# Loads and stores shared by two issuing engines, weight low bits also on GpSimd, and one pair of keys instead of four transposed by TensorE

## The chip, the cores and the metric

The kernel runs on one core of a Trainium2 chip. The core has TensorE (PE, matrix products into PSUM; PEld is its weight load), VectorE (DVE), ScalarE (ACT), GpSimd (POOL) and SyncE (SP), each with its own instruction stream that runs in program order; they wait for each other on semaphores. DMA transfers are issued from the streams of SP, ACT and POOL and carried out by 16 DMA engines. The metric is the device time of one execution in microseconds (us), smaller is better.

## The reference

Block-sparse attention (4 batches, 8 heads, 768 positions, head size 64) is followed by a two-layer network over 3072 tokens:

```python
scores = scale * np.matmul(q, k.transpose(0, 1, 3, 2))      # mask: window, edges, sampled blocks
attn = np.exp(scores - max); attn /= (sum + 1e-09)
x = np.matmul(attn, v)  ->  (3072, 512)
h = x @ w_in                                                # 512 x 2048
g = np.maximum(h, 0.0) + alpha * np.minimum(h, 0.0)
out = g @ w_out                                             # 2048 x 512
```

`moe_w_in` and `moe_w_out` arrive as 64-bit floats (the kernel loads them as pairs of 32-bit words), the rest as 32-bit floats.

## The kernel before, in words

**Precision.** Each operand is written as a sum of two 16-bit floats, a high part (`times`: scale and round) and a low part (`rest`: scale and subtract the high part), and a product is three TensorE products. Before that the 64-bit weights are turned into 32-bit ones in three steps per tile of 128 by 512 (32 tiles, 16 of `w_in`, 16 of `w_out`): `emit_n1` on DVE shifts the high word left by three, `emit_n2` brings in the three low bits, `emit_n3` on DVE merges. `emit_n2` is either one DVE instruction (L813) or one ACT instruction on single bytes (L811).

**Attention.** A unit is one pair of heads for 256 query rows, and it has four score steps (192 in all, 48 units). A step is: scores on PE (`emit_s`, four matmuls, L559), mask and row maximum on DVE (`emit_bias`, L569), exponential on ACT (`emit_exp`, L576), the row sum's reciprocal (L580, L584), the high part of the probabilities P on any of three engines (L348, L350, L352), the low part on POOL in two instructions (L358, L359) or on DVE in one (L356), and a transpose of both parts by one DMA that SP issues (`emit_p_t`, L599). When four steps are done, `emit_av` (36 matmuls, L634) multiplies with V. Keys are transposed too: for the first batch by TensorE (`emit_k_pe`, with copies out of PSUM by `emit_k_copy` on ACT or DVE), for the others by DMA (`emit_k_t`), with a second copy whose halves are swapped (`emit_k_swap`, two DMAs).

**Network.** For each chunk of 256 tokens (12 chunks) there are 8 up groups (`emit_up`, 24 matmuls, L948) and 8 down groups (`emit_down`, 12 matmuls, L987), with the activation on DVE (L958, L959), its high part on ACT (L964) and its low part on POOL (L969). The first down group needs the scale of all of `w_out`, so all its tiles must have gone through the three steps.

**What sets the order.** The kernel lists all operations with a priority, the engines that may do each, a duration guessed for each engine, and the buffers it takes. `Plan.run` plays a list schedule over them: it starts the ready operation of lowest priority number on the engine that would end it first, and lets transfers pass through two rings (SP's and ACT's). The order that comes out is the program order of all engines, and it is fixed. So a changed guess or buffer count moves instructions everywhere. Priorities of the weights are `V_WI`, `W_WI`, `V_WO`, `W_WO` (start and step per tile), of the network `MOE_LAG` and `MOE_BOOST`, of the first values `PL_V` and `P_V`; `BUFS` has the buffer counts; `PL` is a repeating string that says which engine makes the low part of P in a step (`g` POOL, `v` DVE); `LQ` has the engines that may issue loads.

Of the kernel before, what the change touches and what calls it, by code (L numbers as in the profile page):

```python
# [14 lines left out]
ALU = mybir.AluOpType  # L15
# [12 lines left out]
MOE_LAG = 9.585  # L28
MOE_BOOST = 5.593
V_WI = -1.832  # L30
W_WI = 0.74
V_WO = -2.974
W_WO = 1.2
WI_LO = "pe"
PL_V = -24.873
P_V = 3.807
PL = "ggv"
LD = 5
P_PE = 0
RAWP = ["x", "wr"]  # L40
K_PE = 1
Q_PE = 1
BUFS = {"wr": 1, "vf": 4, "qf": 4, "qt": 3, "qn": 2, "ph": 5, "e": 4, "pt": 4, "x": 2, "g": 3, "junk": 2, "sid": 2, "kt": 4, "ks": 4, "v2": 4, "gh": 3, "gl": 3}
# [16 lines left out]
class Plan:  # L60
# [4 lines left out]
    SHARE = {"SP": 0.3, "ACT": 0.7}  # L65
# [15 lines left out]

    def run(self):
        now, left = 0.0, len(self.ops)
        idle = dict.fromkeys(self.ENGINES, 0.0)
# [11 lines left out]
        events = []  # L96
        rings = {"SP": [], "ACT": []}
# [30 lines left out]
        while left:  # L128
            progress = True
            while progress:  # L130
# [4 lines left out]
                for o in ready:  # L135
                    if any(not b.live and all(self.free[x] <= 0 for x in b.pools) for b in o.alloc):
                        continue
# [47 lines left out]
            for _, _, kind, o in due:  # L185
                if kind == "dma":
                    rings["SP" if o.eng == "SP" else "ACT"].append([1.15 * o.dma, o])
                elif kind == "fin":
                    finish(o)
# [5 lines left out]
def attn_moe(ctx: ExitStack, tc: tile.TileContext, q, k, v, sampled, w_in, w_out, alpha, out):  # L195
    nc = tc.nc
# [165 lines left out]
    LQ = {"ACT": 0.06}  # L362
    MAX4 = {"DVE": (0.55, 0), "ACT": 0.85, "POOL": 1.05}
    LOW4 = {"DVE": (0.94, 0), "POOL": (1.05, 1.65)}
# [290 lines left out]
    def prep_k(b, hp, prio, gate, pl):  # L655
# [12 lines left out]
        if b == 0 and K_PE:  # L668
# [7 lines left out]
        o_kt[b, hp] = [plan.op(prio - 2, {"SP": 2.4}, lambda: emit_k_t(b, hp), [o], [kbuf[b, hp]], [nb], dma=2.3)]  # L676
        o_ks[b, hp] = [plan.op(prio - 2, {"SP": 0.12}, lambda e: emit_k_swap(e, b, hp), o_kt[b, hp],
# [21 lines left out]
    def prep_q(c, prio, pl, gate):  # L699
# [16 lines left out]
        for u, fb in zip(us, fbs):  # L716
# [12 lines left out]
            o_qt[u] = plan.op(p - 2, {"SP": 0.8 * f}, lambda u=u: emit_q_t(u), [o], [qtbuf[u]], [nb], dma=0.75 * f)  # L729

    def attend(n):
# [12 lines left out]
        lo = {"POOL": (1.05, 1.65)} if PL[n % len(PL)] == "g" else {"DVE": (0.94, 0)} if PL[n % len(PL)] == "v" else LOW4  # L744
# [10 lines left out]
        o_pt[n] = [plan.op(n - 1, {"SP": 2.4}, lambda: emit_p_t(n), [o], [ptbuf[u, h]], [pb], dma=2.2)]  # L755
# [52 lines left out]
    def emit_n2(e, name, f, h):  # L808
        r, d, byte = raw_of(name, f, h)
        if e == "ACT":  # L810
            nc.scalar.activation(byte[:, :, 4], byte[:, :, 3], AF.Copy, scale=1.0 / 32, bias=-31.0 / 64)  # L811
        else:
            nc.vector.scalar_tensor_tensor(d, low_of(name, f, h), 29, d, ALU.logical_shift_right, ALU.bitwise_or)  # L813
        T["mask", name, f, h] = 7 - (1 << 30) if e == "ACT" else -(1 << 30)
# [291 lines left out]
```

## Time and profile before

| | |
|---|---|
| median of the runs | 878.76 us (fastest 878.57) |
| profiled execution, its own time | 879.08 us |
| its span, first to last instruction | 877.1 us |
| PE / DVE / ACT / POOL busy | 802.9 / 692.0 / 546.0 / 550.2 us |
| mean granted clock of TensorE | 0.963 of full |
| DMA issues on ACT / SP | 136 loads and stores / 248 transposes and 24 swaps |

The profiled execution's own time is 2.0 us more than its span and 0.3 us from the median. The profile cuts the span into 40 slices and gives each engine's busy share of every slice; it lists groups of equal instructions with their mean duration, stretches of time with each engine's busy time, and the instructions in order of time.

### The profile page before, as it was taken

Reading aid. Unit: us, or ns where it says so; the run is one execution under the profiler, and the core shown is the slowest. Engines: PE = TensorE matmul, PEld = TensorE weight load, DVE = VectorE, ACT = ScalarE, POOL = GpSimd, SP = SyncE. Lnnn points to the kernel's source line nnn. Section 1 sums busy time; section 2 is a strip of 40 time slices with the busy share of each in tenths; the row PEclk is TensorE's granted clock in tenths of the full one; section 3 lists DMA queues with packets and bytes.
Section 4 is the critical chain, followed back from the end, with each engine's and each line's share of the span. In section 5 each row is a group of like instructions: output and inputs, shape, how many; then the busy total and the mean of one; then the engine's idle time right before and its main releaser. Section 6 shows DMA issues by size and latency. Waiting matters only on the chain.

```text
span 877.1 us, 17172 instructions
## 1 busy us (share of the span) xinstructions
PE 802.9 (92%) x6249; PEld 534.4 (61%) x6249; DVE 692.0 (79%) x1413; ACT 546.0 (62%) x1178; POOL 550.2 (63%) x446
## 2 busy tenths in 40 slices
PE   3865656899999999999999999999999999999997
PEld 2522323666675666666666667666766766676664
DVE  4999998999887877678888797789797888775322
ACT  5787767678756676765857656477568555564111
POOL 3387556696845877565846776666567666566121
PEclk9876976999999999999999999999999999999999
DMA  7877789576898888977979889777989777766000
GB/s 236 240 180 192 168 180 203 129 134 133 177 208 169 160 149 139 202 140 138 210 157 201 131 145 182 150 140 159 214 151 175 146 133 125 115 125 105 13 25 25
DMA packets 381844, 133.80 MB, mean 153 GB/s; under 512 B 346404, under 2 KB 375104, under 8 KB 381760
## 3 DMA queue, kind: packets, MB, share of 16 engines
q1 hardware_dynamic: 345728, 90.74, 61.2%
q10 hardware_dynamic: 35968, 41.95, 16.3%
q8 instruction: 49, 0.80, 0.4%
q14 instruction: 35, 0.29, 0.1%
q0 software_dynamic: 64, 0.02, 0.0%
HBM read 35.67 MB, written 6.29 MB: 48 GB/s over the span
## 4 chain that ended last, share of the span: by engine, by line
PE 64%; DVE 18%; issue 6%; ACT 3%; DMA 2%; POOL 1%; ACTq 1%; POOLq 0%; DVEq 0%
PE o L987 22%; PE h L948 22%; PE sp L559 11%; PE av L634 9%; DVE e L569 4%; DVE ph L356 2%; DMA kf<-in_k_dram 2%; DVE wo L818 1%; DVE wo L813 1%; ACT e L576 1%; DVE v L356 1%; DVE g L958 1%; DVE wo L356 1%; DVE wo L806 1%; ACT ph L348 1%
## 5 line engine op out<-in xcount | busy, mean ns | idle before, releaser
L948 PE MATMUL h<-x,wi 128*128 128x256 f16 x2304 | 269.4, 274 | 0.0
L948 PEld LDWEIGHTS <-wi 128*128 128x128 f16 x2304 | 225.9, 98 | 39.1 <-issue 1.7
L987 PE MATMUL o<-wo,gh 128*128 128x512 f16 x768 | 229.8, 381 | 1.3 <-DVE wo L356 1.3
L359 POOL TENSOR_TENSOR ph<-e,ph 128x768 f16<-128x768 f32 x128 | 223.0, 1742 | 10.7
L576 ACT ACTIVATE e<-e,nm 128x768 f32<-128x768 f32 x192 | 178.3, 929 | 79.3 <-DVE nm L569 75.1
L569 DVE CUSTOM_DVE_ANT_0 e<-sp,bias,cs 128x768 f32<-128x768 f32 x192 | 190.5, 1007 | 24.7 <-PE sp L559 23.2
L358 POOL TENSOR_SCALAR e<-e,rs 128x768 f32<-128x768 f32 x128 | 134.3, 1049 | 113.9 <-ACT ph L348 63.1
L969 POOL TENSOR_TENSOR gl<-g,gh 128x512 f16<-128x512 f32 x96 | 119.8, 1249 | 101.6 <-ACT gh L964 97.1
L964 ACT CAST gh<-g 128x512 f16<-128x512 f32 x96 | 59.1, 616 | 145.3 <-DVE g L959 128.1
L987 PE MATMUL o<-wo,gl 128*128 128x512 f16 x384 | 146.1, 380 | 1.0 <-POOL gl L969 1.0
L958 DVE TENSOR_SCALAR g<-h,am 128x256 f32<-128x256 f32 x192 | 83.7, 477 | 74.8 <-PE h L948 72.3
L559 PEld LDWEIGHTS <-qt 128*128 128x128 f16 x768 | 74.3, 101 | 90.7 <-issue 36.5
L559 PE MATMUL sp<-kt,qt 128*128 128x512 f16 (+1 forms) x384 | 98.3, 339 | 30.0 <-DVE nm L569 23.7
L987 PEld LDWEIGHTS <-gh 128*128 128x128 f16 x768 | 74.7, 98 | 79.2 <-issue 2.9
L348 ACT ACTIVATE ph<-e,rs 128x768 f16<-128x768 f32 x106 | 97.7, 928 | 15.7 <-DVE rs L584 15.3
L634 PE MATMUL av<-pt,v 128*64 128x256 f16 x1728 | 104.8, 276 | 1.7 <-DVE nm L569 1.7
L634 PEld LDWEIGHTS <-v 128*64 128x64 f16 x1728 | 91.6, 111 | 22.1 <-issue 17.0
L559 PE MATMUL sp<-ks,qt 128*128 128x512 f16 (+1 forms) x384 | 98.7, 340 | 0.0
L356 DVE SCALAR_TENSOR_TENSOR ph<-e,rs,ph 128x768 f16<-128x768 f32 x64 | 82.6, 1291 | 4.9 <-ACT ph L348 4.7
L959 DVE SCALAR_TENSOR_TENSOR g<-h,gsc,g 128x512 f32<-128x512 f32 x96 | 72.1, 751 | 3.4
L987 PEld LDWEIGHTS <-gl 128*128 128x128 f16 x384 | 37.7, 98 | 49.6 <-POOL gl L969 2.8
L352 POOL TENSOR_SCALAR ph<-e,rs 128x768 f16<-128x768 f32 x35 | 35.3, 1008 | 50.7 <-DVE rs L584 37.6
(131 smaller groups left out, 752.1 us busy)
## 6 DMA issues: line engine op xcount, KB each, us to landing
wo<-in_moe_w_in_dram ACTq DMA_DIRECT2D x16, 512.0 KB, 5.8
raw<-in_moe_w_out_dram ACTq DMA_DIRECT2D x16, 512.0 KB, 4.3
kf<-in_k_dram ACTq DMA_DIRECT2D x16, 384.0 KB, 4.6
qf<-in_q_dram ACTq DMA_DIRECT2D x48, 128.0 KB, 3.3
vf<-in_v_dram ACTq DMA_DIRECT2D x16, 384.0 KB, 5.5
out_dram<-ob ACTq DMA_DIRECT2D x24, 256.0 KB, 4.2
ks<-kt SPq DMA_DIRECT2D x24, 192.0 KB, 3.8
pt<-ph SPq DMA_TRANSPOSE x192, 4.1
```

The costliest lines, as they stand in the source:

```text
L348: nc.scalar.activation(dst, src, AF.Copy, scale=scale)
L356: nc.vector.scalar_tensor_tensor(dst, src, scale, hi, ALU.mult, ALU.subtract)
L358: nc.gpsimd.tensor_scalar(tmp, src, scale, 1.0, ALU.mult, ALU.mult)
L359: nc.gpsimd.tensor_tensor(dst, tmp, hi, ALU.subtract)
L559: nc.tensor.matmul(T["sp", n][:, a:z], T["qt", u][:, h, i, :], kt[:, h, a:z], start=(x == 0), stop=(x == 1))
L569: nc.vector.tensor_tensor_reduce(T["e", n], T["sp", n], bias[:, t0 + j % w, :], scale=T["cs", c][:, hp : hp + 1], scalar=3.0e38, op0=ALU.a ...
L576: nc.scalar.activation(T["e", n], T["e", n], AF.Exp, bias=T["nm", n], scale=-1.0, accum_out=T["su", n])
L634: nc.tensor.matmul(av[h * D : (h + 1) * D, : n * P], v2[:, h, t, vv, :], T["pt", u, h][:, pl * NT + t, :], start=(m == 0), stop=(m == len( ...
L948: nc.tensor.matmul(ph[:, i, :], win(w, f, ct), x[:, ct, :], start=(m == 0), stop=(m == len(terms) - 1))
L958: nc.vector.tensor_scalar(g[:, i, :], ph[:, i, :], 0.0, am1[:, f : f + 1], ALU.min, ALU.mult)
L969: nc.gpsimd.tensor_tensor(T["gl", c, j], T["g", c, j], T["gh", c, j], ALU.subtract)
L987: nc.tensor.matmul(T["o", c][t], g[:, i, t * P : (t + 1) * P], wout(w, f), start=(f == 0 and m == 0), stop=(f == NF - 1 and m == 2),)
```

## The change

Four things are changed together.

1. Loads and stores may be issued by SP or by ACT, whichever the planner finds free (before: by ACT alone). Transposes stay on SP.
2. The low bits of a weight tile may also be made on POOL.
3. Only the first of the four key pairs of batch 0 is transposed by TensorE; the other three go by DMA on SP like those of later batches. The probabilities of the first four steps are transposed by TensorE (`P_PE`, before by DMA).
4. The planner's numbers are set anew: priorities, guesses, buffer counts (`wr` 1 to 2, `vf` 4 to 5; `qt` 3 to 2, `ph` 5 to 4, `pt` 4 to 3), and `PL` from "ggv" to "gv", so that every second step instead of every third has its low part of P on DVE.

```diff
-MOE_LAG = 9.585
-MOE_BOOST = 5.593
-V_WI = -1.832
-W_WI = 0.74
-V_WO = -2.974
-W_WO = 1.2
+MOE_LAG = 10.759
+MOE_BOOST = 3.497
+V_WI = -0.008
+W_WI = 0.663
+V_WO = 0.327
+W_WO = 0.625
 WI_LO = "pe"
-PL_V = -24.873
-P_V = 3.807
-PL = "ggv"
+PL_V = -37.055
+P_V = -5.132
+PL = "gv"
-P_PE = 0
-RAWP = ["x", "wr"]
+P_PE = 4
+RAWP = ["wr", "x"]
 K_PE = 1
+N2P = 1.0
...
-    SHARE = {"SP": 0.3, "ACT": 0.7}
+    SHARE = {"SP": 0.5, "ACT": 0.5}
...
-    LQ = {"ACT": 0.06}
+    LQ = {"SP": 0.47, "ACT": 0.5}
...
-        if b == 0 and K_PE:
+        if b == 0 and hp < K_PE:
...
+        elif e == "POOL":
+            nc.gpsimd.tensor_scalar(byte[:, :, 4], byte[:, :, 3], 1.0 / 32, -31.0 / 64, ALU.mult, ALU.add)
...
-        o = plan.op(p, {"ACT": 1.27, "DVE": (0.6, 0)}, lambda e, f=f: emit_n2(e, "wi", f, 0), [o])
+        o = plan.op(p, {"ACT": 1.27, "DVE": (0.65, 0), "POOL": N2P}, lambda e, f=f: emit_n2(e, "wi", f, 0), [o])
...
-            plan.op(stop - MOE_BOOST, {"ACT": 0.06}, lambda e, t=t: emit_store(e, c, t), [o], [], [ob], dma=0.8)
+            plan.op(stop - MOE_BOOST, LQ, lambda e, t=t: emit_store(e, c, t), [o], [], [ob], dma=0.8)
```

The start of ACT's stream before (`kf` are keys, `qf` queries as loaded, `wo<-in_moe_w_in` a raw tile of `w_in`, which is kept in the space of `wo`; `junk` is the output of a sum of squares):

```order
L238 ACTIVATE warm<-ones 128x1
L388 DMA kf<-in_k_dram 128x2x384
L388 DMA qf<-in_q_dram 128x2x128 x4
L388 DMA kf<-in_k_dram 128x2x384 x3
L388 DMA wo<-in_moe_w_in_dram 128x4x256 x5
L344 ACTIVATE junk,kss<-kf 128x768
```

and now:

```order
L251 ACTIVATE warm<-ones 128x1
L401 DMA qf<-in_q_dram 128x2x128 x2
L401 DMA kf<-in_k_dram 128x2x384 x2
L401 DMA wo<-in_moe_w_in_dram 128x4x256 x2
L357 ACTIVATE junk,ssq<-qf 128x256
L357 ACTIVATE junk,kss<-kf 128x768
```

Thirteen issues stood ahead of ACT's first sum of squares, now six do. SP's stream began with twelve transposes of P (`pt<-ph`); now it begins with loads, and the keys' transposes (`kt<-kn`) and swapped copies (`ks<-kt`) stand between further loads:

```order
L401 DMA wo<-in_moe_w_in_dram 128x4x256 x3
L481 DMA_TRANSPOSE kt<-kn 128x12x128
L401 DMA wo<-in_moe_w_in_dram 128x4x256
L401 DMA qf<-in_q_dram 128x2x128
L481 DMA_TRANSPOSE kt<-kn 128x12x128
L401 DMA qf<-in_q_dram 128x2x128 x2
L401 DMA wo<-in_moe_w_in_dram 128x4x256 x4
L401 DMA ks<-kt 64x1536 x2
L481 DMA_TRANSPOSE kt<-kn 128x12x128
```

A load that stands behind a transpose there is issued only after the wait of that transpose. On POOL the first work behind the constants was the high parts of keys, queries and P:

```order
L299 TENSOR_SCALAR nident<-ident 128x128
L352 TENSOR_SCALAR kn<-kf,ks 128x12x64
L352 TENSOR_SCALAR qn<-qf,sq 128x4x64 x2
L352 TENSOR_SCALAR ph<-e,rs 128x768
L358 TENSOR_SCALAR e<-e,rs 128x768
L359 TENSOR_TENSOR ph<-e,ph 128x768
```

and is now the low bits of the first weight tiles (L826, in the space of `wo`):

```order
L312 TENSOR_SCALAR nident<-ident 128x128
L826 TENSOR_SCALAR wo<-wo 128x512 x4
L884 TENSOR_SCALAR sid<-ident,ssc 128x128
L826 TENSOR_SCALAR wo<-wo 128x512
```

Five of the eighteen low-bit operations that POOL does in the new order have moved ahead of its first P.

## Rows read from the trace of the kernel before

**Rows 1.** The page: busy time of each engine; granted clock in 40 slices.

```profile
PE 802.9 (92%) x6249; PEld 534.4 (61%) x6249; DVE 692.0 (79%) x1413; ACT 546.0 (62%) x1178; POOL 550.2 (63%) x446
PEclk9876976999999999999999999999999999999999
```

**Rows 2.** Windows: stretch, length, busy us (instructions) by engine, clock, DMA share, GB/s.

```profile
0.00:24.00 24.00, 9.72 (x69) 6.59 (x70) 11.09 (x43) 13.35 (x28) 8.55 (x26) 1.00 0.74 235
24.00:150.00 126.00, 79.71 (x449) 41.81 (x448) 118.80 (x225) 92.23 (x211) 80.54 (x59) 0.77 0.83 193
150.00:214.00 64.00, 59.64 (x472) 40.31 (x471) 60.48 (x119) 46.28 (x100) 44.14 (x33) 0.95 0.66 132
214.00:840.00 626.00, 621.12 (x5054) 425.08 (x5053) 491.83 (x1012) 389.15 (x834) 410.04 (x323) 1.00 0.83 151
```

**Rows 3.** Timeline of PE: start, duration, instructions; first up group, first down group, 41st step.

```profile
148.82 4.93 PE L948 MATMUL h<-x,wi 128*128 128x256 f16 x24
...
174.10 1.06 PE L987 MATMUL o<-wo,gh 128*128 128x512 f16 x2
...
215.71 0.49 PE L559 MATMUL sp<-kt,qt 128*128 128x512 f16 x2
216.03 0.49 PE L559 MATMUL sp<-ks,qt 128*128 128x512 f16 x2
216.36 2.78 PE L948 MATMUL h<-x,wi 128*128 128x256 f16 x24
```

**Rows 4.** The chain that ended last: start, duration, what; one piece of each kind.

```profile
232.69 2.62 PE h L948 x24
235.96 2.59 PE o L987 x12
238.55 2.09 PE av L634 x36
```

**Rows 5.** Timeline of ACT at the start, with the idle time before in brackets.

```profile
1.10 0.44 ACTq L388 DMA_DIRECT2D kf<-in_k_dram  x1
...
5.21 5.49 ACTq L388 DMA_DIRECT2D wo<-in_moe_w_in_dram  x5
10.75 0.84 ACT L344 ACTIVATE junk<-kf 128x768 bf16<-128x768 f32 x1 [8.46 <-DMA wo<-in_moe_w_in_dram]
```

**Rows 6.** DMA issues: engine, count, KB each, median us from issue to landing.

```profile
kf<-in_k_dram ACTq DMA_DIRECT2D x16, 384.0 KB, 4.6
...
ks<-kt SPq DMA_DIRECT2D x24, 192.0 KB, 3.8
...
kt<-kn SPq DMA_TRANSPOSE x12, 5.1
```

**Rows 7.** Groups by form: shapes, count, busy us, mean ns, idle before.

```profile
L359 POOL TENSOR_TENSOR ph<-e,ph 128x768 f16<-128x768 f32 x128 | 223.0, 1742 | 10.7
...
L358 POOL TENSOR_SCALAR e<-e,rs 128x768 f32<-128x768 f32 x128 | 134.3, 1049 | 113.9 <-ACT ph L348 63.1 <-DVE ph L350 34.2 <-ACT e L576 9.7
...
L356 DVE SCALAR_TENSOR_TENSOR ph<-e,rs,ph 128x768 f16<-128x768 f32 x64 | 82.6, 1291 | 4.9 <-ACT ph L348 4.7
...
L813 DVE SCALAR_TENSOR_TENSOR wo<-raw,wo 128x512 int32<-128x512 int32 x14 | 11.6, 831 | 0.0
...
L813 DVE SCALAR_TENSOR_TENSOR wi<-wo,wi 128x512 int32<-128x512 int32 x11 | 9.0, 828 | 0.0
...
L811 ACT ACTIVATE wo<-wo 128x512 uint8<-128x512 uint8 x5 | 6.8, 1351 | 2.6 <-DVE wi L806 2.6
...
L492 DVE COPY ks<-kp 128x768 f16<-128x768 f16 x6 | 3.3, 554 | 1.2 <-PE kp L484 1.0
...
L352 POOL TENSOR_SCALAR wi<-wi,ssc 128x512 f16<-128x512 f32 x2 | 2.5, 1260 | 4.4 <-PE d L874 4.4
```

**Rows 8.** Timeline of DVE in two places of the first stage.

```profile
54.61 1.05 DVE L818 SCALAR_TENSOR_TENSOR wi<-wo,wi 128x512 int32<-128x512 int32 x1
...
75.10 1.85 DVE L806 TENSOR_SCALAR wi<-wo 128x512 int32<-128x512 int32 x1
76.88 0.68 DVE L818 SCALAR_TENSOR_TENSOR wo<-raw,wo 128x512 int32<-128x512 int32 x1
77.48 0.41 DVE L806 TENSOR_SCALAR wo<-raw 128x512 int32<-128x512 int32 x1
```

**Rows 9.** Timeline of POOL in the same two places.

```profile
54.21 0.91 POOL L358 TENSOR_SCALAR vf<-vf,sv 128x768 f32<-128x768 f32 x1
...
74.73 1.95 POOL L359 TENSOR_TENSOR v<-vf,v 128x768 f16<-128x768 f32 x1
```

More of the change, by code (lines that the diff above doesn't have):

```diff
@@ L80, in op, with room @@
         return o
+    def room(self, o):
+        free = dict(self.free)
+        for b in o.alloc:
+            if b.live:
+                continue
+            pool = next((x for x in b.pools if free[x] > 0), None)
+            if pool is None:
+                return False
+            free[pool] -= 1
+        return True
     def run(self):
         now, left = 0.0, len(self.ops)
-        idle = dict.fromkeys(self.ENGINES, 0.0)
+        idle = dict.fromkeys(self.ENGINES, 1.2)
+        idle["POOL"] = idle["PE"] = idle["DVE"] = 0.0
         kids = {o.n: [] for o in self.ops}
@@ L95, in run @@
         ready = [o for o in self.ops if need[o.n] == 0]
-        events = []
+        events = [(1.2, -1, "idle", None)]
         rings = {"SP": [], "ACT": []}
@@ L135, in run @@
                 for o in ready:
-                    if any(not b.live and all(self.free[x] <= 0 for x in b.pools) for b in o.alloc):
+                    if not self.room(o):
                         continue
@@ L186, in run @@
                 if kind == "dma":
-                    rings["SP" if o.eng == "SP" else "ACT"].append([1.15 * o.dma, o])
+                    rings["SP" if o.eng == "SP" else "ACT"].append([1.05 * o.dma, o])
                 elif kind == "fin":
@@ L361, in attn_moe @@
     T = {}
-    LQ = {"ACT": 0.06}
-    MAX4 = {"DVE": (0.55, 0), "ACT": 0.85, "POOL": 1.05}
-    LOW4 = {"DVE": (0.94, 0), "POOL": (1.05, 1.65)}
+    LQ = {"SP": 0.47, "ACT": 0.5}
+    MAX4 = {"DVE": (0.55, 0), "ACT": 0.85, "POOL": 1.08}
+    LOW4 = {"DVE": (0.94, 0), "POOL": (1.1, 1.7)}
     steps = [(u, j) for u, (c, hp) in enumerate(units) for j in range(2 * chunks[c][2])]
@@ L743, in attend @@
         o = o_hi = plan.op(n - 1, MAX4, lambda e: emit_p_hi(e, n), [o], [pb], [eb])
-        lo = {"POOL": (1.05, 1.65)} if PL[n % len(PL)] == "g" else {"DVE": (0.94, 0)} if PL[n % len(PL)] == "v" else LOW4
+        lo = {"POOL": (1.1, 1.7)} if PL[n % len(PL)] == "g" else {"DVE": (0.94, 0)} if PL[n % len(PL)] == "v" else LOW4
         o = plan.op(n - 1, lo, lambda e: emit_p_lo(e, n), [o], [], [pb, eb])
@@ L811, in emit_n2 @@
             nc.scalar.activation(byte[:, :, 4], byte[:, :, 3], AF.Copy, scale=1.0 / 32, bias=-31.0 / 64)
+        elif e == "POOL":
+            nc.gpsimd.tensor_scalar(byte[:, :, 4], byte[:, :, 3], 1.0 / 32, -31.0 / 64, ALU.mult, ALU.add)
         else:
             nc.vector.scalar_tensor_tensor(d, low_of(name, f, h), 29, d, ALU.logical_shift_right, ALU.bitwise_or)
[L814 removed]
+        T["mask", name, f, h] = -(1 << 30) if e == "DVE" else 7 - (1 << 30)
     def emit_n3(name, f, h):
```

22 lines of the change are left out of this document (11 added, 11 removed).

## The prediction

> **What bounds the kernel now.** I read the page first. PE is busy for 802.9 of 877.1 us, but its granted clock stands at nine tenths or more only from about a fifth of the span on [rows 1]. So there are two stages, and the windows separate them [rows 2]. From 214 to 840 us PE is busy for 621 of 626 us at full clock: there PE is the bound, and only less PE work would help. Up to 214 us DVE is the one that is nearly full: 118.8 of 126 us and 60.5 of 64 us, with PE at 79.7 of 126 us, at a clock of 0.77. Before 24 us DVE has done 11.1 us only. In all, DVE worked 190.4 us of the first 214 and stood idle for 23.6, of which 12.9 lie before 24 us.
>
> What is won must therefore be won in the first 214 us, and paid out by PE later. As a fixed point I take the 41st score step. It starts on PE at 215.7 us [rows 3]; in the order, the DVE step that it needs is the 39th masking step. After it PE still has 88 up groups, 89 down groups, 40 products with V and 152 score steps. At 2.62, 2.59 and 2.09 us [rows 4] and 0.65 us for a step (two rows, 215.71 to 216.36 [rows 3]) that is 230.6 + 230.5 + 83.6 + 98.8 = 643.5 us. 215.7 + 643.5 = 859.2, so 17.9 us are lost later, the drain at the end among them. I keep these 17.9. The forecast is then: when does DVE come to its 39th masking step, and how much PE work is left.
>
> **The start.** ACT issued thirteen loads from 1.10 us on, and its first sum of squares began at 10.75 us after 8.46 us without work [rows 5]. A load of keys issued on the same queue lands after 4.6 us in the median [rows 6], so the first keys could be used from about 5.7 us. With six issues ahead of it instead of thirteen, at 0.5 us (the mean of the first eight, 1.10 to 5.21 us [rows 5]), ACT is free at about 4.2 us. The sum of squares starts 5 us earlier. I take −5; the bounds are −6.5 (free at 4.2) and 0, if the later keys, which all pass the same DMA engines, become the wait.
>
> **DVE's work up to the 39th masking step.** Counted over the order with the mean durations by form, 219.6 us become 215.4. The kinds:
> - low bits of the weights: 25 instructions become 8, 17 x 0.83 = −14.1 us (L813 [rows 7]); 18 tiles go to POOL.
> - low part of P: 12 become 18, 6 x 1.291 = +7.7 (L356 [rows 7]).
> - copies of transposed keys: 9 become 4, −2.8, and 2 copies of transposed P, +1.1, all at 0.554 (L492 [rows 7]).
> - everything else, counted alike: +3.9 (two more low parts of V and of the output weights, more high parts of queries and P, fewer of `w_in`).
>
> The sum is −4.2. Instructions follow each other with some overlap: 219.6 us of durations were 190.4 us of busy time [rows 2], a factor of 0.87, so −3.7 us on the clock.
>
> **How POOL and DVE hinder each other.** A DVE shift takes 0.41 us alone, and 1.85 us while POOL's subtraction of 1.95 us runs; a merge takes 0.68 alone and 1.05 beside a POOL multiplication that ends at 55.1 us [rows 8, 9]. Up to the fixed point POOL has 35 subtractions in the order before and 26 now. I give each half of the longest delay, 0.7 us: −6.3. The 18 low-bit operations are new on POOL; beside a multiplication I saw 0.37, and most of them don't meet a DVE instruction of that kind, so 0.2 us each: +3.6. The term is −2.7. Its bounds are −13 (9 x 1.44, new ones free) and +9 (last but one rival).
>
> **Keys by DMA, P by TensorE.** PE loses 108 small matmuls and gains 48; PE is idle there for 46 of 126 us [rows 2], so 0. The three transposes take 5.1 us to land and the swapped copies 3.8 [rows 6], about 9 us in a chain. They are hidden: the fifth score step, the first that needs the second pair, now stands on PE behind the first product with V. If that cover goes, the price is one such chain, 9 us.
>
> **After the fixed point.** The order now leaves 90 down groups instead of 89: +2.6 us. 26 further low parts of P go to DVE, 26 x 1.29 = 34 us; DVE is idle for 626 − 492 = 134 us there [rows 2], so 0, and POOL gets 2.8 us back for each (L358, L359 [rows 7]). Loads issued by SP cost ACT nothing any more and DMA the same; 0.
>
> **Sum.** −5 − 3.7 − 2.7 + 2.6 = −8.8 us, on the span 877.1 to 868.3. The profiled execution's own time is 0.3 us from the median, so I put it against the median: 878.76 − 8.8 = **870.0 us**.
>
> **The rivals.**
>
> *The relief pays in full.* The first down group, not the 41st step, may be what counts: it starts at 174.1 us [rows 3] and needs all output weights. Counted over the order, DVE's work up to the second low part of the output weights falls from 174.7 to 156.4 us, 18.4 x 0.87 = 16 us, and the first down group stands behind 28 score steps and 3 up groups instead of 31 and 5, so 7.2 us more are left for PE. −16 − 5 − 6.3 + 7.2 = −20: 859 us. For it: PE may do score steps later, in its backlog. Against: DVE is full until 214 us [rows 2] and has to do the postponed steps as well.
>
> *Given back in the steady stage.* With four buffers for P instead of five and three for transposed P instead of four, the order has on average 18.0 us of PE work between a unit's last score step and its product with V, before 20.7. If that makes PE wait only 0.25 us in each of the 40 units left, 10 us are gone: 880. Against: PE is hardly ever idle there, 5 of 626 us [rows 2].
>
> *POOL's low bits hold DVE up wholly.* If each of the 18 blocks DVE as a subtraction does, 0.7 us instead of 0.2, the term −2.7 becomes +6.3: 879. The rows show a block beside both kinds, shorter beside the multiplication [rows 8, 9]. The Trainium skill's page "SBUF — State Buffer", section "SBUF: two separate sides", has it that the port pair shared by the two engines is an exclusive lock, and that the one that comes second is blocked wholly. The rows agree that there is a block; how often it strikes they don't settle.
>
> *Slower: POOL is slow at single bytes.* No row shows POOL on bytes. The nearest: POOL takes 1.26 us for 512 columns of floats, and ACT 1.35 us for the same bytes (L352, L811 [rows 7]); I take 1.3. DVE merges a tile in its fixed place, so it waits if POOL isn't done. Counted over the order (times 0.87), DVE has 1.7 to 12 us of work between shift and merge of the 18 tiles, in thirteen of them under 3.3 us. With 0.2 us for a handover each way (my choice) nothing is lost at 1.3 us. At 2.6 us the waits add up to 8.7 us and eat the whole gain: that is the point from which it decides. At 4.0 us they are 26 us, and the time is 896 or more.
>
> **How the numbers follow.** The likeliest case, the sum, gets 0.45; relief in full 0.22; blocked by POOL 0.13; given back 0.12; slow bytes 0.08. A measurement of this kernel tells from no change about 2%, 17.6 us: faster means under 861.2, slower over 896.3. Relief in full lies under 861.2, and of the sum's case a little, if its bounds −6.5 and −13 meet; so faster 0.24. Of slow bytes, and of a lost cover of 9 us on top of two of the others, slower 0.07. Within 2%: 0.69. The range goes from 852, where relief in full and a free POOL meet, to 888, where POOL takes 3.2 us for its bytes or the keys' chain is bare on top of a blocked DVE; about 1 in 10 is left out on either side. Of the sum alone it would be 863 to 876.
>
> **What would show it.** ACT's first sum of squares at 5 to 6 us, and the first down group before 168 us. DVE busy for over 93% between 24 us and the 41st step, and that step at 204 to 208 us. POOL's low-bit instructions near 1.3 us, and no merge on DVE whose idle time ends with POOL. PE idle for less than 8 us between that step and 830 us. I am wrong if DVE shows idle time that ends with a DMA of keys or weights, since SP issues loads only behind its transposes' waits, or if the products with V wait for transposed P.

## The result, and the profile of the changed kernel

The changed kernel takes 869.6 us in the median, the kernel before 878.7 us in the same measurement. The ratio is 0.9894, with a 95% interval of 0.9877 to 0.9911. It is about 1% faster, within the 2% called "same". The forecast was 870.0 us. The profiled execution of the changed kernel has a span of 866.9 us and took 868.9 us; before it was 877.1 us of span, so 10.2 us are gone from it. (One of the four executions of each took over 2.8 ms; without it the medians are 868.9 and 878.6 us, and the ratio leaves it out.)

The page, with busy times and the granted clock in 40 slices, answers to [rows 1]:

```profile
PE 795.1 (92%) x6189; PEld 534.9 (62%) x6189; DVE 700.6 (81%) x1424; ACT 542.7 (63%) x1176; POOL 492.4 (57%) x402
...
PEclk9677778999999999999999999999999999999999
```

The windows answer to [rows 2], with the same columns (stretch, length, PE, PEld, DVE, ACT, POOL busy with counts, clock, DMA share, GB/s):

```profile
0.00:24.00 24.00, 12.65 (x72) 7.20 (x73) 13.02 (x51) 15.70 (x33) 8.00 (x24) 1.00 0.96 283
24.00:150.00 126.00, 76.59 (x423) 45.51 (x422) 120.78 (x216) 93.51 (x216) 88.53 (x65) 0.76 0.79 192
150.00:214.00 64.00, 58.25 (x471) 40.07 (x470) 62.39 (x120) 48.11 (x101) 44.95 (x34) 0.97 0.73 149
214.00:840.00 626.00, 625.65 (x5091) 428.85 (x5090) 497.87 (x1028) 381.54 (x823) 346.27 (x277) 1.00 0.80 149
```

The two stages are still there. DVE is fuller up to 214 us, 196.2 us against 190.4, and PE fills 625.65 of the 626 us behind, where it filled 621.12.

The timeline of PE answers to [rows 3]: first up group, first down group, 41st score step.

```profile
145.25 2.78 PE L963 MATMUL h<-x,wi 128*128 128x256 f16 x24
...
157.25 0.59 PE L1002 MATMUL o<-wo,gh 128*128 128x512 f16 x2
...
207.95 0.49 PE L572 MATMUL sp<-kt,qt 128*128 128x512 f16 x2
```

The 41st step comes 7.8 us earlier (before 215.71). The first down group comes 16.9 us earlier (before 174.10).

The start of ACT answers to [rows 5]:

```profile
4.68 1.96 ACTq L401 DMA_DIRECT2D wo<-in_moe_w_in_dram  x2
6.69 0.42 ACT L357 ACTIVATE junk<-qf 128x256 bf16<-128x256 f32 x1 [4.41 <-issue]
```

The first sum of squares is at 6.69 us instead of 10.75.

The groups by form, of the low bits on POOL (L826) and, up to 205 us, of the shift on DVE ahead of them (L819), answer to [rows 7]:

```profile
L826 POOL TENSOR_SCALAR wo<-wo 128x512 uint8<-128x512 uint8 x11 | 16.9, 1537 | 25.7 <-DVE wi L819 25.6
L826 POOL TENSOR_SCALAR raw<-raw 128x512 uint8<-128x512 uint8 x7 | 12.1, 1726 | 7.2 <-DVE wo L819 3.8 <-DVE rs L597 3.5
...
L819 DVE TENSOR_SCALAR wo<-raw 128x512 int32<-128x512 int32 x16 | 11.8, 740 | 0.4 <-DMA raw<-in_moe_w_out_dram 0.4
L819 DVE TENSOR_SCALAR wi<-wo 128x512 int32<-128x512 int32 x16 | 10.9, 700 | 0.0
```

POOL needs 1.54 to 1.73 us for 512 bytes, and the shift that costs DVE 0.41 us alone takes 0.70 to 0.74 us in the mean.

**The balance.** At the 41st step 7.8 us are won. PE then has 90 down groups left instead of 89 (+2.6 us). Work left by the prediction's count is 646.1 us, and 866.9 − 207.95 − 646.1 = 12.9 us are lost later, where 17.9 us were lost before (−5.0). Together −7.8 + 2.6 − 5.0 = −10.2 us.

About 1.5 us of this division come from TensorE's clock just ahead of the 41st step. In the changed kernel it was granted at half (1.2 GHz) from 202.6 to 206.0 us, after PE had waited 2.27 us for a mask. In the run below with the low bits on DVE, which has the same order and the same wait there, it stayed at full (2.4 GHz). These are the window and the up group in it, first of the changed kernel, then of that run:

```profile
202.60:206.00 3.40, 3.40 (x18) 2.40 (x16) 3.40 (x6) 2.84 (x8) 3.27 (x2) 0.50 0.85 154
203.42 4.04 PE L963 MATMUL h<-x,wi 128*128 128x256 f16 x24
```

```profile
203.10:206.50 3.40, 3.40 (x32) 2.90 (x30) 3.40 (x6) 2.84 (x8) 3.26 (x2) 1.00 0.82 153
203.51 2.78 PE L964 MATMUL h<-x,wi 128*128 128x256 f16 x24
```

The 41st step comes 2.60 us behind the 39th masking step in the first and 1.05 us in the second, and yet from the masking step to the end both take 661.5 us. So I also read the balance from the masking step, which the forecast was about (213.70 before, 205.35 now): −8.4 + 2.6 − 4.4 = −10.2 us. The forecast had −11.4, +2.6 and 0. So the total was right by two errors that nearly cancel: 3.0 us too much hoped for in the first stage, and 4.4 us not seen behind it.

### The profile page after: what moved, and what is told of

Same layout as the page of the kernel before. It is cut to its first block, busy times and chain, and to the rows that moved or that the text cites. A ratio compares the mean times of both kernels' runs of the same rounds, so it can differ in the third digit from the quotient of the medians.

```text
span 866.9 us, 17068 instructions
## 1 busy us (share of the span) xinstructions
PE 795.1 (92%) x6189; PEld 534.9 (62%) x6189; DVE 700.6 (81%) x1424; ACT 542.7 (63%) x1176; POOL 492.4 (57%) x402
## 4 chain that ended last, share of the span: by engine, by line
PE 72%; DVE 19%; issue 5%; DMA 2%; POOL 1%; ACT 0%; POOLq 0%; DVEq 0%; ACTq 0%
PE h L963 25%; PE o L1002 24%; PE sp L572 12%; PE av L647 10%; DVE e L582 3%; DVE ph L369 3%; DVE wi L833 1%; DMA raw<-in_moe_w_out_dram 1%; DVE wo L833 1%; DVE wi L819 1%; DVE wo L819 1%; DVE wo L369 1%; DVE qn L440 1%; DVE g L973 1%; DMA al_r<-in_moe_alpha_dram 1%
## 5 line engine op out<-in xcount | busy, mean ns | idle before, releaser
L371 POOL TENSOR_SCALAR e<-e,rs 128x768 f32<-128x768 f32 x96 | 97.4, 1015 | 164.9 <-DVE ph L363 85.3
L372 POOL TENSOR_TENSOR ph<-e,ph 128x768 f16<-128x768 f32 x96 | 168.1, 1751 | 8.0
L369 DVE SCALAR_TENSOR_TENSOR ph<-e,rs,ph 128x768 f16<-128x768 f32 x96 | 114.3, 1190 | 5.4 <-ACT ph L361 4.5
L647 PE MATMUL av<-pt,v 128*64 128x256 f16 x1728 | 108.0, 281 | 10.0 <-DVE nm L582 10.0
L647 PEld LDWEIGHTS <-v 128*64 128x64 f16 x1728 | 94.7, 113 | 24.5 <-issue 22.5
L361 ACT ACTIVATE ph<-e,rs 128x768 f16<-128x768 f32 x99 | 91.5, 927 | 9.8 <-DVE rs L597 8.1
L365 POOL TENSOR_SCALAR ph<-e,rs 128x768 f16<-128x768 f32 x34 | 40.2, 1183 | 52.5 <-DVE rs L597 52.4
```

What stands on the lines that cost most here:

```text
L361: nc.scalar.activation(dst, src, AF.Copy, scale=scale)
L369: nc.vector.scalar_tensor_tensor(dst, src, scale, hi, ALU.mult, ALU.subtract)
L371: nc.gpsimd.tensor_scalar(tmp, src, scale, 1.0, ALU.mult, ALU.mult)
L372: nc.gpsimd.tensor_tensor(dst, tmp, hi, ALU.subtract)
L647: nc.tensor.matmul(av[h * D : (h + 1) * D, : n * P], v2[:, h, t, vv, :], T["pt", u, h][:, pl * NT + t, :], start=(m == 0), stop=(m == len( ...
```

## The experiments

All times were measured beside the kernel before (878.5 to 878.7 us in the three sessions). This table gives for each kernel the start of the 39th masking step on DVE and of the 41st score step on PE, the loss behind that step (span, less the step's start, less PE's work left counted as in the prediction), the span, and the median.

| kernel | 39th masking | 41st step | loss later | span | median |
|---|---|---|---|---|---|
| before | 213.7 | 215.7 | 17.9 | 877.1 | 878.7 |
| changed | 205.4 | 208.0 | 12.9 | 866.9 | 869.6 (868.9) |
| before, 7 early loads by SyncE | 208.2 | 210.2 | 17.2 | 870.8 | 873.6 |
| changed, all loads by ACT | 211.9 | 214.5 | 12.9 | 873.4 | 874.6 |
| changed, low bits on DVE | 205.9 | 206.9 | 14.4 | 867.4 | 868.4 |
| changed, low bits left out | 199.5 | 202.1 | 12.1 | 860.2 | 862.1 |
| changed, P's low part as before | 204.9 | 205.9 | 14.1 | 866.1 | 869.3 |
| changed, alpha late | 203.3 | 205.9 | 12.8 | 864.8 | 867.7 |
| alpha late, 9 low bits on ACT | 202.3 | 203.3 | 14.8 | 864.2 | 866.0 |
| the same, no weights by ACT at the start | 204.7 | 207.3 | 12.5 | 865.9 | 867.8 |
| the same, 10 high parts of P on ACT | 199.3 | 200.4 | 12.9 | 859.3 | 861.2 |
| changed, 4 buffers for keys and V | 215.1 | 216.2 | 14.7 | 874.4 | 877.1 |
| changed, lag and boost as before | 204.7 | 209.8 | 16.5 | 867.2 | 869.4 |
| before, key norms later on PE | 214.6 | 216.7 | 31.5 | 891.6 | 893.7 |

In the order of the changed kernel the 41st step depends on the clock ahead of it. The clock was at half there for 3.4 us, and the step 2.60 us behind the masking step, in the changed kernel and in the runs with all loads by ACT, low bits left out, alpha late, and no weights by ACT at the start. It was at full, and the distance 1.05 us, in those with low bits on DVE, P's low part as before, 9 low bits on ACT, and 10 high parts on ACT. A late step makes the loss behind it look smaller by as much. So I read the first stage from the masking step, and compare losses at a like clock only. Unless said otherwise, a run keeps the planned order of its parent and changes only the engine or the place named.

### The start alone

```diff
-        o.fn(o.eng)
+        if o.dma is not None and set(o.alts) == {"ACT"}:
+            nld += 1
+        eng = "SP" if o.dma is not None and set(o.alts) == {"ACT"} and nld <= 14 and nld % 2 == 0 else o.eng
+        o.fn(eng)
```

> The kernel before with its planned order, where seven of the first fourteen loads (two of queries, two of keys, two of weights, one of V) are issued by SyncE instead of ScalarE; nothing else changes. ACT then issues seven loads before its first sum of squares instead of thirteen, which begins near 7 us instead of 10.75. Theory (the start counts one for one): DVE's first real work comes about 3 us earlier and so does the 41st step: 212.7 us, time 875.7 (before 878.7). Rival 1, the whole difference that the run with all loads on ACT showed (6.5 us) comes from the start: time 872. Rival 2, that difference comes from later loads, and the start is of no account: 878.7.

873.6 us, ratio 0.9941 (0.9927 to 0.9955). The start of ACT in this run:

```profile
2.60 0.49 ACTq L388 DMA_DIRECT2D kf<-in_k_dram  x1
4.88 2.32 ACTq L388 DMA_DIRECT2D wo<-in_moe_w_in_dram  x3
7.24 0.84 ACT L344 ACTIVATE junk<-kf 128x768 bf16<-128x768 f32 x1 [4.96 <-DMA kf<-in_k_dram]
```

ACT begins 3.5 us earlier, and the masking step comes 5.5 us earlier. So the seven loads alone give more than half of what the change gave. The first 23 masking steps all come 3.3 to 3.4 us earlier, one for one with ACT as the theory had it. The other 2.1 us are won later, 1.8 of them ahead of the 24th step, where DVE had waited for a load of output weights. The shift there, before:

```profile
148.56 1.42 DVE L806 TENSOR_SCALAR wo<-raw 128x512 int32<-128x512 int32 x1 [1.03 <-DMA raw<-in_moe_w_out_dram]
```

And in this run:

```profile
144.12 0.79 DVE L806 TENSOR_SCALAR wo<-raw 128x512 int32<-128x512 int32 x1
```

That load took 7.3 us from issue to landing before and 6.2 us here; whether the seven early loads have a part in that isn't shown. Up to the masking step DVE is busy for 191.35 us here and 190.07 before, and idle for 16.8 us against 23.6: the start takes idle time away, not work.

### All loads by ACT

```diff
-        o.fn(o.eng)
+        eng = "ACT" if o.dma is not None and set(o.alts) == {"SP", "ACT"} else o.eng
+        o.fn(eng)
```

> The changed kernel with its planned order, but every load and store that may go by either engine is issued by ACT again; weights, keys and P as in the change. Theory (the start of ACT and DVE sets when the 41st score step comes, and PE does the rest): ACT issues 13 loads before its first sum of squares instead of 6, so this begins near 10.7 us instead of 6.7; the 41st step moves from 208.0 to about 211 us, the loss after it stays near 12.9 us, and the time is about 872.5 us (changed kernel 869.6). Rival 1, the second queue also won the 5 us after that step: the keys of the next batch are again late for PE, the loss goes back to 17.9 us, and the time is about 877.5. Rival 2, the start is of no account: 869.6.

874.6 us, ratio 0.9953 (0.9935 to 0.9971): 5.0 us slower than the changed kernel (5.7 against 868.9). The masking step comes 6.5 us later, more than the 3.8 us by which ACT's first sum of squares is late (10.47 us against 6.69). The loss later is 12.9 us, unchanged to a tenth, so rival 1 falls: the second queue has no part in the 5 us won behind the 41st step. The part of the 6.5 us that is not the start is in the timeline of ACT:

```profile
27.80 0.61 ACTq L401 DMA_DIRECT2D qf<-in_q_dram  x1
28.22 0.18 ACT L589 ACTIVATION_READ_ACCUMULATOR e<-e,nm 128x1 f32 x1
34.66 0.37 ACTq L401 DMA_DIRECT2D qf<-in_q_dram  x1
35.13 0.43 ACTq L401 DMA_DIRECT2D wo<-in_moe_w_in_dram  x1
35.60 0.84 ACT L357 ACTIVATE junk<-vf 128x768 bf16<-128x768 f32 x1 [7.19 <-DMA kt<-kn]
```

ACT stands still for 7.2 us. Two things hold it, both in the trace's times of landing. V, of which it wants the sum of squares, was issued at 21.98 us and landed at 32.85. And the load of queries ahead of that sum waits longer still. The loads and transposes take eight semaphores in turn; this load has the one that SyncE's first transpose of keys used, which was issued at 21.41 us and landed at 34.64, and it went out at 34.66. In the changed kernel the same V landed 5.5 us after its issue, the transpose 6.8 us after, at 26.52, and ACT came to its load at 26.54, so nobody waited.

### POOL's low bits: on DVE, and left out

```diff
 def emit_n2(e, name, f, h):
+    e = "DVE" if e == "POOL" else e
```

> The changed kernel with its planned order, but the 18 low-bit operations that POOL took are done by DVE, each at its place in the order; loads, keys and P as in the change. Theory (DVE's work bounds the first stage, POOL's operations hinder it by 0.2 us each): 18 x 0.83 = 14.9 us more on DVE, times 0.87 = 13.0, less 3.6 of hindrance: the 41st step 9.4 us later at 217.4 us, time about 879. Rival 1, each of POOL's operations blocks DVE wholly (0.7 us each, 12.6 in all): the two cancel, 41st step at 208.4, time about 870. Rival 2, DVE is not the bound: within 1 us of 869.6 with the 41st step unmoved.

868.4 us, ratio 0.9883 (0.9862 to 0.9903), no slower than the changed kernel. The second run leaves the operation out:

```diff
         elif e == "POOL":
-            nc.gpsimd.tensor_scalar(byte[:, :, 4], byte[:, :, 3], 1.0 / 32, -31.0 / 64, ALU.mult, ALU.add)
+            pass
```

> The changed kernel with its planned order, with POOL's 18 low-bit operations left out: three low bits of 18 weight tiles are not moved into place, so this work is missing from the time; nothing takes its place. It measures what these operations cost the others. Theory (0.2 us of hindrance each, and a merge on DVE that waited for POOL 0.6 us): the 41st step about 4 us earlier, at 204 us, time about 865.5. Rival 1, each blocks DVE wholly, 0.7 us: 12.6 us, 41st step at 195.4, time 857. Rival 2, they cost DVE nothing: 869.6.

862.1 us, ratio 0.9809 (0.9787 to 0.983). The windows up to the masking step show why; first the changed kernel, then low bits on DVE, then left out:

```profile
0.00:205.35 205.35, 139.30 (x905) 87.04 (x906) 188.80 (x370) 152.69 (x339) 133.11 (x116) 0.84 0.80 193
```

```profile
0.00:205.85 205.85, 137.75 (x917) 87.46 (x918) 188.71 (x388) 152.08 (x339) 106.42 (x98) 0.85 0.80 192
```

```profile
0.00:199.45 199.45, 139.61 (x904) 86.97 (x905) 176.16 (x369) 151.92 (x339) 106.06 (x98) 0.90 0.84 198
```

DVE does 18 instructions more in the second row and is busy as long as in the first. In the third it does as many as in the first and is busy 12.6 us less. So each operation on POOL cost DVE 12.6 / 18 = 0.70 us, as rival 1 had it, and DVE's own low bits cost it 0.71 to 0.74 us (its rows there): POOL saved DVE nothing. Of the 12.6 us, 6.2 are on the 32 shifts (22.7 us become 16.5) and 2.9 on the 32 merges (27.4 become 24.5). Only 5.9 us reached the masking step, since DVE's idle time rose from 16.6 to 23.3 us; behind the start its longest waits were now for scores (3.5 us), for PE's sums of the weights' squares (3.1) and for a load of output weights (2.7). So the time lies between the 865.5 of the theory and the 857 of rival 1. DVE is the bound of the first stage with little in hand.

How one such operation strikes, in the changed kernel. DVE's timeline:

```profile
93.11 0.42 DVE L819 TENSOR_SCALAR wo<-raw 128x512 int32<-128x512 int32 x1
93.45 0.68 DVE L833 SCALAR_TENSOR_TENSOR wi<-wo,wi 128x512 int32<-128x512 int32 x1
94.05 1.62 DVE L819 TENSOR_SCALAR wi<-wo 128x512 int32<-128x512 int32 x1
95.59 0.41 DVE L819 TENSOR_SCALAR wo<-raw 128x512 int32<-128x512 int32 x1
```

And POOL's:

```profile
93.61 1.78 POOL L826 TENSOR_SCALAR raw<-raw 128x512 uint8<-128x512 uint8 x1 [0.45 <-DVE wo L819]
```

The shift of one tile releases POOL. The shift of the next tile, 0.6 us later, takes 1.62 us instead of 0.41 and ends 0.28 us behind POOL's end: it hardly got on while POOL ran. POOL's operation, which began beside a merge on DVE, took 1.78 us, and the shortest of the 18 took 1.33. The order itself makes them meet, since DVE does the shift of the next tile while POOL does the low bits of the last. The Trainium skill's page "SBUF — State Buffer", section "SBUF: two separate sides", has the port pair that the two share as an exclusive lock for a whole instruction; the 1.62 us beside 0.41 us agree with it. That page's list leaves ACT out of the lock, which the runs with work moved to ACT bear out below.

### P's low part back to POOL

```diff
 def emit_p_lo(e, n):
+    e = ("POOL", "POOL", "DVE")[n % 3] if n < 40 else e
```

> The changed kernel with its planned order, but the low parts of P of the first 40 score steps go to POOL and DVE by the pattern of the kernel before (two to POOL, one to DVE), which moves 7 of them net from DVE to POOL. Theory 1, the prediction's own terms (DVE saves 7 x 1.29 x 0.87 = 7.9 us, POOL's subtractions hinder it by 0.7 us each, 4.9): the 41st step 3 us earlier at 205 us, time 866.6. Theory 2, a subtraction on POOL holds a DVE instruction beside it by as much as DVE would need to do the low part itself (2.19 us beside one, 1.01 us alone, in the trace of the changed kernel): 7 x 1.0 saved, 7 x 1.2 lost, 41st step at 208 to 209.5, time 869.6 to 871.

869.3 us, ratio 0.99 (0.9881 to 0.9918). The masking step moves by 0.5 us, the 41st step by 2.0 (1.5 of them are the clock, at full here), and the time not at all. Seven low parts less on DVE lowered its busy time by 1.8 us only (186.97 against 188.80): 7 x 1.29 x 0.87 = 7.9 us saved, 6.1 taken back. By the masking step and the time, theory 2 holds. Each multiplication and subtraction on POOL took back 0.87 us, where the prediction had 0.7.

### Alpha's transpose behind the start

```diff
-    for o in plan.run():
+    order = plan.run()
+    late = [o for o in order if o.n in (o_alp.n, o_al.n)]
+    order = [o for o in order if o not in late]
+    at = order.index(o_gsc)
+    for o in order[:at] + late + order[at:]:
```

> The changed kernel with one move in its planned order: the transpose of alpha on PE and the subtraction behind it on DVE stand directly ahead of the operation that first uses alpha, instead of first on both engines. In the changed kernel DVE's first real work is that subtraction; it waits 8.2 us for PE, which waits 9.0 us for the load of alpha, and begins at 9.3 us. Theory (the start of DVE counts in full): DVE begins at about 7.3 us with the first square's result, 2 us earlier, the 41st step comes at 206 us, time about 867.5. Rival, the first score steps wait for something else (mask, keys), and the start of DVE is slack: 869.6, with the first score step still at 20.6 us.

867.7 us, ratio 0.9877 (0.9857 to 0.9897), 2.0 us less than the changed kernel, as expected. (It is 1.3 us against 868.9, and the two intervals overlap, so the gain rests on the traces.) DVE's first work in the changed kernel was the subtraction of alpha:

```profile
9.30 0.17 DVE L906 TENSOR_SCALAR al<-pa 128x16 f32<-128x16 f32 x1 [8.23 <-PE pa L796]
```

It now starts with the first scale of the queries:

```profile
6.81 0.15 DVE L349 TENSOR_SCALAR uq<-ssq 128x1 int32<-128x1 int32 x1 [5.74 <-ACT junk L357]
```

2.5 us are won there, 2.0 us at the masking step and 2.1 us of span. At its new place the subtraction makes DVE wait 3.1 us for PE; at the last masking step ahead of it DVE was 3.9 us early. So the gain at the start reaches the end, less what the new place costs.

### Half of the low bits on ACT

This and the next two build on the run with alpha late.

```diff
 def emit_n2(e, name, f, h):
+    if e == "POOL":
+        n2p.append(f)
+        e = "ACT" if len(n2p) % 2 == 0 else "POOL"
```

> The changed kernel with alpha's transpose moved back as in the run before, and every second of POOL's 18 low-bit operations done by ACT at its place in the order. Theory (an operation of POOL costs DVE about a third of a microsecond net, one of ACT nothing, and ACT is busy only three quarters of the first stage): 9 x 0.33 = 3 us earlier at the 41st step, which comes at 203 us, time about 864.7 (with alpha moved alone 867.65). Rival (ACT's 9 x 1.35 = 12 us delay what it hands to DVE and POOL): 41st step at 206 or later, time 868 or more.

866.0 us, ratio 0.9848 (0.9834 to 0.9861). The 41st step comes 2.6 us earlier, near the 3 us expected, but 1.5 of them are the clock, at half ahead of it with alpha late and at full here. The masking step comes only 1.1 us earlier, and the time falls by 1.7 us. DVE's busy time to the masking step falls by 7.2 us, 0.8 us for each of the nine operations, but its idle time rises by 6.2.

### No weights issued by ACT at the start

```diff
+    early = [o for o in order if o.dma is not None and o.eng == "ACT" and o.dma == 1.6][:2]
...
+        eng = "SP" if o in early else o.eng
```

> The run with alpha moved back and nine low-bit operations on ACT (865.98 us), and ACT's two loads of weights ahead of its first sum of squares issued by SyncE at their places in the order. These two waited until the first two loads of queries had landed (4.95 and 5.83 us), since the loads share eight semaphores. Theory (the start counts at least one for one): ACT's first sum of squares at 5.0 instead of 6.3 us, the 41st step 1.3 to 2 us earlier, time about 864.3. Rival (the next keys land at 8.1 us whatever ACT does, and the gain ends there): 866.

867.8 us, ratio 0.9884 (0.9867 to 0.9901): 1.8 us slower instead of faster. ACT's first sum of squares does start at 4.71 us, but then ACT stands still as it did with all loads on ACT:

```profile
29.51 0.38 ACTq L401 DMA_DIRECT2D qf<-in_q_dram  x1
29.93 0.84 ACT L357 ACTIVATE junk<-vf 128x768 bf16<-128x768 f32 x1 [5.13 <-DMA kt<-kn]
```

V was issued at 17.11 us and landed at 28.40; the first transpose of keys was issued at 16.79 and landed at 29.49, and ACT's load, with the same semaphore, went out at 29.51. Neither theory had this: 5.1 us of ACT's standing still ate the 1.6 us at the start. The bytes moved show the place. Here is GB/s in 40 slices of 0.6 us from 16 to 40 us, in the run with alpha late and nothing else:

```profile
GB/s 388 385 382 391 386 382 361 218 165 131 126 295 262 176 249 370 362 402 331 65 59 213 291 211 282 272 341 381 382 393 410 364 365 372 389 388 235 150 104 33
```

And in this run:

```profile
GB/s 391 391 385 387 382 386 378 321 183 82 50 79 117 74 229 222 148 101 119 83 68 41 312 364 386 362 296 291 323 328 254 275 348 364 346 347 271 304 365 355
```

While the first transposes run, from about 20.5 us on, the rate stands below 300 GB/s for 4.8 us in the first row, and after a rise for 4.2 us again; in the second row it does so for 8.4 us in one piece, down to 41. Why the transposes take longer here than there, these runs don't tell.

### High parts of P on ACT too

```diff
 def emit_p_hi(e, n):
+    e = "ACT" if e == "POOL" and n < 40 else e
```

> The kernel of the run before, and the high parts of P of the first 40 score steps that POOL did are done by ACT. Theory (an operation of POOL on 768 columns holds DVE by about 0.3 us, and ACT does it in 0.92 instead of 1.56 us): 41st step 3 us earlier again, time about 861.5. Rival (ACT, with 12 us of low bits and 10 us of high parts more, becomes late with its exponentials): 41st step no earlier, time 865 or more.

861.2 us, ratio 0.9816 (0.9792 to 0.984). It beats both kernels, and the run before it by 6.6 us. Here are the windows to the masking step of the run before it and of this one:

```profile
0.00:204.72 204.72, 136.88 (x908) 86.89 (x909) 181.13 (x369) 161.64 (x348) 120.05 (x107) 0.81 0.84 193
```

```profile
0.00:199.29 199.29, 138.80 (x920) 88.18 (x921) 174.80 (x370) 168.51 (x357) 103.12 (x97) 0.84 0.86 199
```

POOL does ten instructions less, DVE is busy 6.3 us less, 0.63 us for each, and 5.4 us of it reach the masking step. ACT took them at 168.5 busy us of 199 without becoming the bound. It still stands behind the first transpose of keys, for 3.9 us here and 5.1 in the run before, so up to 1.2 us of the gain may be that.

### What the second stage won: buffers, numbers, key norms

Two runs were planned anew, so their whole order differs, and one moves a single kind of step. First the number of buffers for loaded keys and V:

```diff
-BUFS = {"wr": 2, "vf": 5,
+BUFS = {"wr": 2, "vf": 4,
```

> The changed kernel planned anew with four buffers for loaded keys and V instead of five. In its order the loads of the next batch's keys stand behind score steps 46, 48, 48, 48, 91 and so on, and the key norm on PE behind steps 47, 48, 48, 49, 92; in the changed kernel the loads stand behind steps 34, 41, 44, 45, 81 and the norms behind 38, 43, 45, 49, 87. Theory (the 5 us that PE no longer loses after the 41st step are the waits for keys that were loaded too late, and the fifth buffer took them away): the key norm waits come back, the loss after the 41st step goes from 12.9 to 16 to 18 us, time 873 to 875 if the 41st step stays at 208. Rival (the loss fell for another reason, such as the numbers that place the up and down groups): it stays within 1 us of 12.9, and the time differs from 869.6 only by what the 41st step moves.

877.1 us, ratio 0.9989 (0.9976 to 1.0002). The masking step is 9.8 us later, and PE has one down group less to do behind the 41st step (−2.6). The loss later is 14.7 us, below the theory's 16 to 18, although the keys are loaded as late as before. The clock was at full ahead of the 41st step here, and three of the four runs in the changed order with such a clock have 14.1 to 14.8 (the fourth 12.9): at a like clock the loss hasn't risen. And the waits of PE behind the 41st step name no key norm at all:

```profile
PE sp L572 <- DVE nm L582: 1.2, 2, 0.6
PE sp L572 <- DVE x L663: 0.7, 1, 0.7
```

In the kernel before, PE waited 2.7 us in three key norms there. So late keys alone don't make these waits, and the theory falls. Then the two numbers that place the up and down groups:

```diff
-MOE_LAG = 10.759
-MOE_BOOST = 3.497
+MOE_LAG = 9.585
+MOE_BOOST = 5.593
```

> The changed kernel planned anew with the two numbers that place the up and down groups (lag 9.585, boost 5.593) of the kernel before. The loads of the next batch's keys stand as early as in the changed kernel for the third and fourth batch, and later (behind steps 33, 47, 47, 48) for the second. Theory (early keys won the 5 us after the 41st step): the loss there goes from 12.9 to about 14 us, by the second batch alone. Rival (the two numbers won them): the loss goes back to about 17.9 us.

869.4 us, ratio 0.989 (0.9876 to 0.9903). The loss goes to 16.5 us, with the clock at full ahead of the step too: some 2 us above those three runs, and below 17.9. But PE has two down groups less to do behind the 41st step, so the time is the same. The waits are of another kind than before again, score steps that wait for DVE:

```profile
PE sp L572 <- DVE nm L582: 1.8, 3, 0.9
PE sp L572 <- DVE x L663: 1.6, 2, 0.9
```

Last, in the kernel before, the key norms on PE go behind the next long group; here order is the planned order, and norms holds the scale behind each norm:

```diff
+    for sc in norms:
+        nm = sc.deps[0]
+        at, sa = order.index(nm), order.index(sc)
+        nxt = next(i for i in range(at + 1, len(order)) if order[i].eng == "PE" and order[i].alts["PE"] > 2)
...
+            order[at : end + 1] = [o for o in order[at : nxt + 1] if o not in (nm, sc)] + [nm] + ...
```

> The kernel before with one kind of move in its planned order: the ten key norms on PE and the scale behind each on DVE, for all key loads of the second, third and fourth batch whose place allows it, stand behind the next up group, down group or product with V on PE instead of ahead of it. In the kernel before, three of these norms made PE wait 2.7 us for the sum of squares on ACT, which starts in the moment the keys land. Theory (these waits are part of the 5 us that the change won after the 41st step): the waits are gone, the loss after the 41st step goes from 17.9 to about 15.2 us, time 876.0 (before 878.7). Rival (the wait only moves to the score step that needs the keys): 878.7.

893.7 us, ratio 1.0174 (1.0152 to 1.0195): 15 us slower. All twelve norms moved on PE, not ten, and the scale behind each kept its place in DVE's own row of instructions, other than I had meant. So DVE now stands at the scale until the norm comes. The waits behind the 41st step, first of DVE, then of PE:

```profile
DVE ku L336 <- PE tot L445: 19.8, 9, 3.3
```

```profile
PE sp L559 <- DVE nm L569: 6.1, 5, 1.9
PE sp L559 <- DVE x L650: 5.4, 4, 2.4
```

DVE waits 19.8 us there (1.6 us in the kernel before), and the maskings and products behind it come late for PE. The run does not tell what the 2.7 us are worth. It shows something else: DVE has well over 100 us to spare in this stage, and a wait of 2 us at the wrong place on it still reaches PE.

## Why the prediction came out, step by step

**Two stages, and the 41st step as the fixed point: right, with a flaw.** In the runs that keep the changed kernel's order, what the masking step gained came out in the span within 0.8 us: −5.9 and −6.6 with low bits left out, −2.0 and −2.1 with alpha late, +6.5 and +6.5 with all loads on ACT. Only with ten high parts on ACT did 6.1 us become 7.6. The 41st step itself moved by a further 1.55 us with the clock, which the span didn't show.

**The start, −5: right in size, not in its mechanism.** The seven loads alone gave −5.5 at the masking step, but only 3.4 of it stand from the first masking step on; the rest was won later, which I hadn't counted. ACT came 4.1 us earlier, not 5, and at 6.69 us, not at 5 to 6. I had reckoned 0.5 us for an issue and no wait. The ninth load of the two engines waits until the first has landed, and so on: ACT's two weights went out at 4.68 and 5.57 us, each 0.02 us after the landing of the load that had its semaphore, and the second issue took 1.08 us. DVE's own start moved by 2.8 us only, since it stood behind alpha's load. The rest came as idle time that DVE no longer had behind 24 us: in all it fell from 23.6 us to 16.6. The Trainium skill's page "DMA: Bandwidth & Descriptors", section "Issuing engines are not separate DMA queues", has it that a second issuing engine saves only the sequencer's time, usually little. Here ACT's time for issues stood ahead of everything else, and what seven of them cost was not little: 3.4 us at the first masking step, 5.0 us of time (873.6 against 878.6 us).

**DVE's work −3.7 and the hindrance −2.7: this step failed.** Together −6.4 were forecast; DVE's busy time to the masking step went from 190.07 to 188.80, −1.3, and the whole step, less the start, by 8.4 − 5.5 = 2.8 us. The failing term is "0.2 us each" for POOL's low bits. Left out, they gave back 0.70 us each: 12.6 us instead of 3.6, which eats the 14.1 us of low bits that DVE no longer does (12.3 us with the factor of 0.87). The 0.37 us I had seen beside one multiplication and the thought that most would meet no DVE instruction of that kind were wrong: the order sets the next tile's shift right beside them, and 6.2 of the 12.6 us are on shifts. The subtractions were sized a little low, 0.87 us with their multiplication instead of 0.7. The low parts of P on DVE were too: 18 took 26.4 us, where 12 had taken 15.8 (+10.6 instead of +7.7). The sizes don't add up to what was measured (−3.7 − 7.8 + 12.6 = +1.1 us without the last, −1.3 measured), so over 2 us are not accounted for. The bound of +9 was the change of the term by the rival; the term itself would be +6.3.

**Keys by DMA, 0: the cover held.** The fifth score step started at 59.55 us, behind the first product with V at 56.3, and no wait of PE names transposed keys. But the transposes can cost elsewhere what I had not listed: in three of the runs ACT stood 7.2, 5.1 and 3.9 us, for V that landed late beside them and for a semaphore shared with one. In the changed kernel it happened not to.

**After the fixed point, +2.6: right. The 17.9 us kept: wrong.** 12.9 us are lost now, and 14.1 to 14.8 in three of the four runs of this order with the clock at full ahead of the 41st step: 3 to 4 us of the 5.0 are a gain, the rest is the clock. Of PE's gaps over 0.15 us behind the 41st step, 5.5 us before, 1.4 us are left (2.9 to 3.4 in those three runs); the three key norms (2.7 us) and a score step (1.2 us) are the largest that went. The second queue has no part in it (12.9 us without it), nor the start (17.2 us with it), nor POOL's low bits (12.1 without them). At a like clock four buffers bring nothing of the loss back (14.7) and the two numbers some 2 us (16.5), each in a new order with other waits. Which feature of the order takes the waits away stays open.

**The rivals.** *Relief in full*: the first down group came 16.9 us earlier, not the 27 us that its terms make (16 + 5 + 6.3), and paid nothing beyond the 41st step; its sign "before 168 us" was there without its time, so the sign did not tell the cases apart. *Given back*: the loss fell instead. *POOL holds DVE up wholly*: the mechanism is the one that happened, at 0.70 us; the time it gave, 879, didn't come, since the later stage gave 4.4 us and the first, read from the masking step, 6.0 us more than it allows. Of these the start makes 0.5 (5.5 instead of 5) and the nine subtractions 1.5 (at 0.87 us instead of 0.7); the rest the runs don't divide. *Slow bytes*: 1.54 to 1.73 us in the mean, beyond the 1.3 I took and below the 2.6 where it would decide; the shortest took 1.33 us, so the size without DVE beside it was right; one merge waited, 0.6 us.

**The other signs.** DVE was busy for 175.8 of the 181.4 us from 24 us to the masking step, 97%; the 41st step at 208.0 lies at the edge of 204 to 208; PE's gaps over 0.15 us from there to 830 us sum to 0.8 us. Up to the masking step, DVE's idle time that ended with a load of weights is 0.4 us, and no product with V waited for transposed P.

## What to carry to other kernels

Work moved from DVE to POOL need not relieve DVE: here 18 low-bit operations and 7 low parts changed sides with no change of the time, while 19 operations moved from POOL to ACT, with alpha and two loads moved at the start, made 861.2 us of 869.6. Price such a move by DVE's busy time with the operation left out, not by the busy time of the engine that takes it. And a sum that comes out right may hold two wrong terms: compare each term with the trace, the fixed point first. Here that one, a step on PE, also moved with the clock just ahead of it.

## What the runs showed of the hardware that I had not expected

- Loads and transposes of both issuing engines take eight semaphores in turn. With alpha late, the ninth to thirteenth load of the two engines went out at 4.51, 4.97, 5.42, 5.85 and 6.42 us, and the first five had landed at 4.49, 4.95, 5.40, 5.83 and 6.41. So a load on ACT can also wait for a transpose on SyncE: in two runs it went out 0.02 us after the transpose had landed, some 5 and 6 us after ACT's work ahead of it had ended.
- Early in the kernel a transpose of keys took 6.8 us from issue to landing in the changed kernel, and 12.7 and 13.2 us in two of the runs, and V beside it 11 us; the 5.1 us of [rows 6] were a median over the whole run. Beside transposes the bytes moved fell from some 380 GB/s to between 126 and 295 in the first 4.8 us with alpha late, and to between 41 and 229 in the run without weights by ACT.
- The load of alpha, 8 KB issued by POOL at about 2.3 us, landed 6.6 us later and held DVE's start back.
